# Hedgehog linear attention, twice and mixed: phase 2 with token-major queries, a DMA exchange and 32x32 array tiles

## The chip, the cores and the metric

The kernel runs on one core of one Trainium2 chip. The metric is the time of one execution on the device in microseconds; lower is better. Engines are called as in the profile: PE (TensorE matmuls), PEld (its weight loads), DVE (VectorE), ACT (ScalarE), POOL (GpSimd) and SP (SyncE, which here only issues DMAs).

## The reference, cut to what matters

Two linear attentions, A and B, run over the same input x of 2048 tokens and 448 features, with 16 heads of 28 features each. The outputs are mixed by a gate per token.

```python
def _ref(x, wqkv, w_phi, wo):                 # once with A's weights, once with B's
    q, k, v = split(x @ wqkv)                 # each (heads, tokens, 28)
    pq = einsum("hsd,hdf->hsf", q, w_phi);  pk = einsum("hsd,hdf->hsf", k, w_phi)
    phi_q = concat([softmax(pq), softmax(-pq)]);  phi_k = concat([softmax(pk), softmax(-pk)])
    kv = einsum("hsf,hsd->hfd", phi_k, v);  z = einsum("hsf->hf", phi_k)
    num = einsum("hqf,hfd->hqd", phi_q, kv)
    den = einsum("hqf,hf->hq", phi_q, z)[..., None] + 1e-6
    return merge_heads(num / den) @ wo
g = sigmoid((x * gate_w).sum(-1, keepdims=True))
out = g * a + (1 - g) * b
```

## The kernel before, in words

Everything is 32-bit. x lies transposed in SBUF (features on partitions, tokens along the free axis) as a high and a low part, and so do the projection weights, so that a product is a sum over 11 chunk pairs: seven with the high weights, four with the low ones. w_phi is folded into the k and q weights first (`fold`), so the projections give pk and pq at once. The tokens are cut into 16 tiles of 128.

The order of the work is written out by hand: each engine runs its instructions in the order in which the program lists them, and waits on semaphores for the others. Nothing is rescheduled.

**Phase 1**, for each tile t: k projection (`proj`, 22 matmuls of 448 columns: tokens on the output's partitions), the two softmaxes on DVE, ACT and POOL (`k_soft`: shift by the maximum and the minimum, exponentials, sums, reciprocals, products), v projection with the gate's logit as an extra column (`v_out`), and the accumulation of phi_k^T v of the tile before (`kv_acc`). In `kv_acc` the outputs of four heads lie on the four column strips of the array (29 rows each at partitions 0, 32, 64, 96), and all sums stay in one PSUM bank over the 16 tiles. The q weights are folded in tiles 6 to 9, wo is loaded in tile 11.

**Phase 2** makes q feature-major: `q_mm` takes the weights as the stationary operand (128 padded features, 32 to a head, four heads to a block) and 256 tokens as the moving one. A unit is two such blocks for 256 tokens, 44 matmuls for the two units of a tile; `q_shift` turns it by 32x32 blocks on DVE, reduces, and POOL subtracts; `q_done` is the exponential (ACT) and the turn back (DVE, into eT). `num` multiplies eT by the block-diagonal kvbd, four heads at a time, 8 matmuls for each of A and B, with 30 columns a head: 28 numerators, the sum for the denominator, and the softmax's own sum. `weigh` and `combine` work out the weights (DVE), multiply the numerators (DVE) and add the two halves (POOL). `out_turn` turns the result by seven TensorE transposes, `out_split` makes its high and low parts (ACT, DVE), `out_mm` is the output projection of 21 matmuls of 448 columns, `out_end` copies and stores. Tile t's loop body holds the q units of a later tile, the numerators of tile t, and the output of tile t - 1.

PSUM has eight banks: two of one bank (`one`), and in phase 1 three of two banks (`two`), which phase 2 gives to the numerators and the transposes. The DMAs all go through SP's queue, in program order.

Of the kernel before, what the change touches and what calls it, by code (L numbers as in the profile page):

```python
# [23 lines left out]
TB = 256  # L24
MC = 30
WARM = 16


@with_exitstack
def hedgehog_mix(ctx: ExitStack, tc: tile.TileContext, xd, wv, wkt, wqt, wphi, wo, cmask, cpmask, out):  # L30
# [9 lines left out]
    ident = const.tile([P, P], F32, name="ident")  # L40
    make_identity(nc, ident)
    mask = const.tile([PF, 4], F32, name="mask")
    pmask = const.tile([P, 4], F32, name="pmask")
    xg = [const.tile([P, 7, GT], F32R, name=f"xg{g}") for g in range(NG)]
    glog = const.tile([P, NT], F32, name="glog")
    gate = const.tile([P, NT, 2], F32, name="gate")

    work = ctx.enter_context(tc.tile_pool(name="work", bufs=2))
    wt_pool = ctx.enter_context(tc.tile_pool(name="wt", bufs=1, side="right"))
    start = ExitStack()  # L50
    raw = start.enter_context(tc.tile_pool(name="raw", bufs=1, side="right"))
    ph1 = ExitStack()
    wk_pool = ph1.enter_context(tc.tile_pool(name="wkv", bufs=1))
    wp = wk_pool.tile([PF, 2, 4, HP], F32, name="wp")
    bd = wk_pool.tile([PF, 2, 4, P], F32, name="bd")
    wkh = wk_pool.tile([P, 4, 2 * D], F32R, name="wkh")
    wkl = wk_pool.tile([P, 4, 2 * D], F32R, name="wkl")
    wvh = wk_pool.tile([P, 4, VC], F32R, name="wvh")
    wvl = wk_pool.tile([P, 4, VC], F32R, name="wvl")
    NV = 3  # L60
    vs = [wk_pool.tile([P, 2, NP, 2, DH + 1], F32, name=f"vs{i}") for i in range(NV)]


# [17 lines left out]
    def load_wt(src, n):  # L81
        wt = wt_pool.tile([P, 4096], F32, name="wt")[:PF].rearrange("p (b g c) -> p b g c", b=2, g=4)
        for c in range(0, 512, n):
            for b in range(2):
                nc.sync.dma_start(wt[:, b, :, c:c + n], src[b, :, c:c + n].rearrange("(g p) c -> p g c", p=PF))  # L85
        return wt
# [15 lines left out]
    load_x_rest(0, P, 2 * P, GT)  # L102
    nc.sync.dma_start(pmask, cpmask)
    for v in vs:
        nc.gpsimd.memset(v[:, :, :, :, DH:], 1.0)
    for q in range(4):
        nc.vector.tensor_scalar(bd[:, :, :, q * HP:(q + 1) * HP], wp, mask[:, q:q + 1], None, op0=OP.mult)

    def fold(c, wt, wh, wl, w):
        n = 4 * w  # L110
        ps = two.tile([P, 2, 512], F32, name="two")
        for b in range(2):
            for g in range(4):
                nc.tensor.matmul(ps[:, b, g * n:(g + 1) * n], wt[:, b, g, c * P:(c + 1) * P],  # L114
                                 bd[:, b, g].rearrange("p (q f) -> p q f", f=HP)[:, :, :w], start=True, stop=True)
        dh = wh[:, c, :].rearrange("p (b f) -> p b f", b=2)
        dl = wl[:, c, :].rearrange("p (b f) -> p b f", b=2)
        nc.scalar.activation(dh, ps[:, :, :4 * n], AF.Copy)
        nc.vector.tensor_tensor(dl, ps[:, :, :4 * n], dh.bitcast(F32), OP.subtract)

    def proj(t, wh, wl, name, widths):
        ps = two.tile([P, 2, 512], F32, name="two")
# [15 lines left out]
    def shift(ps):  # L138
        p4 = hb(ps[:, :, :D])
        mx = wk_pool.tile([P, 2, 2, H], F32, name="mx", bufs=2)  # L140
        e = wk_pool.tile([P, 2, HA * DH], F32, name="e", bufs=2)
# [8 lines left out]
    def expo(e):  # L150
        for s in range(2):
            nc.scalar.activation(e[:, s], e[:, s], AF.Exp)  # L152
        return e

    def k_soft(ps):
        e = expo(shift(ps))
        sm = wk_pool.tile([P, 2, HA], F32, name="sm", bufs=2)
        rs = wk_pool.tile([P, 2, HA], F32, name="rs", bufs=2)
# [14 lines left out]
    kvp = one.tile([P, 512], F32, name="one")  # L173
    nc.vector.memset(kvp, 0.0)
    kvp = kvp[:, :HA * DH // 2].rearrange("p (b g s f) -> p b g s f", b=2, g=4, f=DH)
# [310 lines left out]
```

## Time and profile before

| what | value |
|---|---|
| time, median of 3 runs | 416.81 us (415.45 to 416.84) |
| profiled execution: time | 416.56 us |
| profiled execution: span | 414.5 us |
| busy PE, PEld, DVE, ACT, POOL | 404.6, 380.6, 308.3, 124.9, 187.5 us |
| granted TensorE clock | 0.996 of full speed |
| DMA | 15.62 MB, 38 GB/s on average |

The span runs from the program's first instruction to its last; the time is taken from outside and is some 2 us longer. Busy times are the union of an engine's instructions. In a row of a group the columns are line, engine, operation, output<-inputs with the shapes, the count, then after the first bar the busy time in us and the mean duration of one in ns, and after the second bar the idle time of the engine just before and what ended it. A row of the chain has start and length in us, engine, tile and line. A row of a window has, per engine, the busy us and the number of instructions, then the granted clock, the DMA share and GB/s.

### The profile page before, as it was taken

Reading aid. Unit: us, or ns where it says so; the run is one execution under the profiler, and the core shown is the slowest. Engines: PE = TensorE matmul, PEld = TensorE weight load, DVE = VectorE, ACT = ScalarE, POOL = GpSimd, SP = SyncE. Lnnn points to the kernel's source line nnn. Section 1 sums busy time; section 2 is a strip of 40 time slices with the busy share of each in tenths; the row PEclk is TensorE's granted clock in tenths of the full one; section 3 lists DMA queues with packets and bytes.
Section 4 is the critical chain, followed back from the end, with each engine's and each line's share of the span. In section 5 each row is a group of like instructions: output and inputs, shape, how many; then the busy total and the mean of one; then the engine's idle time right before and its main releaser. Section 6 shows DMA issues by size and latency. Waiting matters only on the chain.

```text
span 414.5 us, 8240 instructions
## 1 busy us (share of the span) xinstructions
PE 404.6 (98%) x3536; PEld 380.6 (92%) x3536; DVE 308.3 (74%) x453; ACT 124.9 (30%) x162; POOL 187.5 (45%) x159
## 2 busy tenths in 40 slices
PE   8999999999999999999799999999999999999996
PEld 7898888899998888899699999999999999999995
DVE  2776666666676666678899987888788878888961
ACT  2624242423332222225432322132213221322212
POOL 0375565643321333338865636443644364436321
PEclk9999999999999999999989999999999999999999
DMA  8845306000000000000000000000000000000001
GB/s 182 287 130 150 103 2 252 7 2 2 2 2 2 2 2 2 2 0 3 1 2 22 24 0 24 24 22 2 24 23 24 0 24 24 23 2 24 23 24 44
DMA packets 12036, 15.62 MB, mean 38 GB/s; under 512 B 880, under 2 KB 9056, under 8 KB 12000
## 3 DMA queue, kind: packets, MB, share of 16 engines
q1 hardware_dynamic: 12000, 15.10, 11.7%
q8 instruction: 28, 0.46, 0.5%
q14 instruction: 8, 0.07, 0.1%
HBM read 11.43 MB, written 3.67 MB: 36 GB/s over the span
## 4 chain that ended last, share of the span: by engine, by line
PE 86%; DVE 6%; ACT 2%; POOL 2%; DMA 2%; SPq 1%; issue 1%; POOLq 0%; DVEq 0%; ACTq 0%
PE two L130 34%; PE one L240 17%; PE one L371 16%; PE nb L323 6%; PE na L323 6%; PE one L184 3%; PE turn L354 3%; PE two L114 2%; DMA xraw<-in_xt 2%; DVE eT L262 1%; SPq L85 1%; DVE ctt L347 1%; DVE sm L160 1%; DVE qmx L250 0%; ACT wt L258 0%
## 5 line engine op out<-in xcount | busy, mean ns | idle before, releaser
L164 POOL TENSOR_TENSOR e<-e,rs 128x896 f32<-128x896 f32 x32 | 53.8, 1703 | 92.9 <-DVE rs L161 92.9
L349 POOL TENSOR_TENSOR o<-ctt 128x448 f32<-128x448 f32 x32 | 36.3, 1152 | 76.1 <-PE one L371 49.3
L152 ACT ACTIVATE e<-e 128x896 f32<-128x896 f32 x32 | 30.2, 955 | 106.7 <-DVE e L146 106.6
L240 PE MATMUL one<-xg,wqh 128*128 128x256 f32 x392 | 56.8, 285 | 0.0
L130 PE MATMUL two<-wkh,xg 128*128 128x448 f32 x224 | 52.5, 372 | 0.7 <-POOL xg L79 0.4
L142 DVE TENSOR_REDUCE mx<-two 128x32 f32<-128x896 f32 x16 | 17.5, 1091 | 47.8 <-PE two L130 47.8
L240 PEld LDWEIGHTS one<-xg,wqh 128*128 128x128 f32 x392 | 52.3, 193 | 0.4
L130 PE MATMUL two<-wvh,xg 128*128 128x450 f32 (+1 forms) x224 | 51.4, 369 | 0.0
L253 POOL TENSOR_TENSOR wt<-wt,qmx 128x512 f32<-128x512 f32 x32 | 33.6, 1049 | 32.4 <-DVE qmx L250 32.4
L130 PEld LDWEIGHTS two<-wkh,xg 128*128 128x128 f32 x224 | 40.8, 188 | 5.5 <-POOL xg L79 0.7
L130 PEld LDWEIGHTS two<-wvh,xg 128*128 128x128 f32 x224 | 42.4, 189 | 3.7
L358 ACT ACTIVATE oh<-turn 128x896 fp32r<-128x896 f32 (+2 forms) x17 | 14.8, 873 | 101.0 <-DVE cdd L336 79.2
L262 DVE STREAM_TRANSPOSE eT<-wt 128x1024 f32<-128x1024 f32 x32 | 39.4, 1233 | 2.1 <-ACT wt L258 2.1
L258 ACT ACTIVATE wt<-wt 128x1024 f32<-128x1024 f32 x32 | 32.5, 1052 | 12.6 <-POOL wt L254 12.6
L240 PE MATMUL one<-xg,wql 128*128 128x256 f32 x224 | 36.0, 283 | 0.0
L160 DVE TENSOR_REDUCE sm<-e 128x32 f32<-128x896 f32 x32 | 33.3, 1081 | 1.3
L323 PE MATMUL nb<-kvbd,eT 128*128 128x120 f32 x256 | 31.4, 275 | 2.7 <-DVE eT L262 2.7
L254 POOL TENSOR_TENSOR wt<-qmx,wt 128x512 f32<-128x512 f32 x32 | 33.5, 1048 | 0.0
L323 PEld LDWEIGHTS nb<-kvbd,eT 128*128 128x128 f32 x256 | 29.9, 192 | 2.9 <-DVE eT L262 2.9
L323 PE MATMUL na<-kvbd,eT 128*128 128x120 f32 x256 | 31.2, 275 | 0.3 <-POOL kvbd L310 0.3
L130 PE MATMUL two<-wvl,xg 128*128 128x450 f32 (+1 forms) x128 | 31.4, 367 | 0.0
L130 PE MATMUL two<-wkl,xg 128*128 128x448 f32 x128 | 31.1, 364 | 0.0
(75 smaller groups left out, 686.7 us busy)
## 6 DMA issues: line engine op xcount, KB each, us to landing
out<-ob SPq DMA_DIRECT2D x16, 224.0 KB, 1.9
xraw<-in_xt SPq DMA_DIRECT2D x3, 1024.0 KB, 5.5
wvr<-in_wv SPq DMA_DIRECT2D x4, 449.0 KB, 6.8
wt<-in_wkt SPq DMA_DIRECT2D x8, 224.0 KB, 5.5
wt<-in_wqt SPq DMA_DIRECT2D x2, 896.0 KB, 9.5
wor<-in_wo SPq DMA_DIRECT2D x1, 1568.0 KB, 10.4
xraw<-in_xt SPq DMA_DIRECT2D x2, 256.0 KB, 7.3
xraw<-in_xt SPq DMA_DIRECT2D x1, 512.0 KB, 8.6
```

Of the source, the lines that this page charges most:

```text
L130: nc.tensor.matmul(ps[:, b, :n], x[:, xc, o:o + P], w[:, wc, lo:lo + n], start=i == 0, stop=i == len(terms) - 1)
L152: nc.scalar.activation(e[:, s], e[:, s], AF.Exp)
L160: nc.vector.tensor_reduce(sm[:, s], e[:, s].rearrange("p (h f) -> p h f", f=DH), AX.X, OP.add)
L164: nc.gpsimd.tensor_tensor(e3, e3, rs[:, s, :, None].to_broadcast([P, HA, DH]), OP.mult)
L240: nc.tensor.matmul(ps[:, i * TB:(i + 1) * TB], w[:, wc, lo:lo + P], x[:, xc, o:o + TB], start=n == 0, stop=n == len(terms) - 1)
L253: nc.gpsimd.tensor_tensor(ep[:, :512].rearrange("p (j f) -> p j f", f=HP), t3, bc[0], OP.subtract)
L254: nc.gpsimd.tensor_tensor(ep[:, 512:].rearrange("p (j f) -> p j f", f=HP), bc[1], t3, OP.subtract)
L258: nc.scalar.activation(ep, ep, AF.Exp)
L262: nc.vector.transpose(eT.rearrange("p s i t -> p (s i t)"), ep)
L323: nc.tensor.matmul(ps[:, s, g * 120:(g + 1) * 120], eTs[t // 2, 2 * b + g // 2][:, s, g % 2, o:o + P], kvbd[:, b, s, g].rearrange("p h m - ...
L349: nc.gpsimd.tensor_tensor(o[:, (lo + b) * D:(lo + b + 1) * D], tt[:, 0].rearrange("p a f -> p (a f)"), tt[:, 1].rearrange("p a f -> p (a f ...
L371: nc.tensor.matmul(ps[:, :D], a, w, start=first and i == 0, stop=last and i == len(terms) - 1)
```

## The change

Phase 2 is rebuilt, and with it the hand-over from phase 1.

- q is projected like k: tokens on partitions, 22 matmuls of 448 columns a tile (`proj` into `qps`). `q_shift` subtracts the maximum, into uq.
- `q_swap` exchanges partitions and head groups: 16 DMAs from SBUF to SBUF, each 32 partitions of 896 bytes. After it partition 32r + j holds head group r of the tokens 32c + j, c along the free axis. uq has one buffer, the target tq two.
- `q_exp0` and `q_exp1` (ACT) and `q_min` (DVE, POOL) make the two softmaxes' exponentials; `q_turn` turns 32x32 blocks on DVE, so that features lie on partitions, 32 to a head group.
- `num` runs in 32x32 tiles of the array: for each of A and B, each softmax, each column strip g and each row strip r a matmul of 32 rows, 32 columns and 128 tokens. Its 64 outputs fill four PSUM banks, row strip r in bank r. There is no block-diagonal kvbd any more.
- `n_turn` turns all of it back on DVE; `n_rec` and `n_mix` work out the weights, with the products and the sum on POOL; `o_turn` turns the result on DVE (before: TensorE transposes); `o_hi` and `o_lo` split it on ACT and POOL. The heads now lie in another order, so wo's rows are permuted once by two DMAs within DRAM (wos) and loaded in seven parts at the end of phase 1.
- The gate is exchanged as q is, by 16 small DMAs for tiles 0 to 12 and 16 for the last three.
- q projections run four tiles ahead (LEAD): tiles 0 and 1 in phase 1's tiles 12 and 13, tiles 2 and 3 behind phase 1. The q weights are folded in tiles 2 to 5. Buffers are shared over the phases, and vs has two buffers instead of three.

The core of the diff, with the new functions:

```diff
@@ kv_acc
-                    h = 4 * g + r
+                    h = 4 * r + g
@@ new
+    def q_shift(k, ps):
+        mx = work.tile([P, 2, H], F32, name="qmx")
+        p4 = hb(ps[:, :, :D])
+        nc.vector.tensor_reduce(mx, p4, AX.X, OP.max)
+        for b in range(2):
+            nc.vector.tensor_tensor(uq[:, :, b], p4[:, b].rearrange("p (r g) f -> p r g f", r=4),
+                                    mx[:, b].rearrange("p (r g) -> p r g", r=4)[:, :, :, None].to_broadcast([P, 4, 4, DH]),
+                                    OP.subtract)
+    def q_swap(k):
+        tr = trs[k] = tq[k % 2]
+        for r in range(4):
+            for c in range(4):
+                nc.sync.dma_start(tr[32 * r:32 * r + 32, c], uq[32 * c:32 * c + 32, r])
+    def q_exp0(k):
+        nc.scalar.activation(eq[:, 0, :, :, :DH], tview(k), AF.Exp)
+    def q_min(k):
+        mn = work.tile([P, 4, 8], F32, name="qmn")
+        nc.vector.tensor_reduce(mn, trs[k].rearrange("p c b g f -> p c (b g) f"), AX.X, OP.min)
+        nc.gpsimd.tensor_tensor(eq[:, 1, :, :, :DH], mn.rearrange("p c a -> p a c")[:, :, :, None].to_broadcast([P, 8, 4, DH]),
+                                tview(k), OP.subtract)
+    def q_exp1(k):
+        nc.scalar.activation(eq[:, 1, :, :, :DH], eq[:, 1, :, :, :DH], AF.Exp)
+    def q_turn(k):
+        eT = wtb[:, 2048 * (k % 2):2048 * (k % 2) + 2048]
+        eTs[k] = eT.rearrange("p (s b g t) -> p s b g t", s=2, b=2, g=4)
+        nc.vector.transpose(eT, eq.rearrange("p s a c f -> p (s a c f)"))
+    def gates(lo, hi):
+        gl = glog[:, lo:hi]
+        nc.scalar.activation(gl, gl, AF.Exp, scale=-1.0)
+        nc.vector.tensor_scalar(gl, gl, 1.0, None, op0=OP.add)
+        nc.vector.reciprocal(gl, gl)
+        for r in range(4):
+            for c in range(4):
+                nc.sync.dma_start(gate[32 * r:32 * r + 32, 0, c, lo:hi], glog[32 * c:32 * c + 32, lo:hi])
+        nc.gpsimd.tensor_scalar(gate[:, 1, :, lo:hi], gate[:, 0, :, lo:hi], -1.0, 1.0, op0=OP.mult, op1=OP.add)
@@ phase 1, in the loop over t (tile 0: the rows of wo are permuted in DRAM)
+            w5 = wos.rearrange("g (r b f) n -> b g r (f n)", r=4, b=2)
+            for b in range(2):
+                nc.sync.dma_start(w5[b], wo[b * D:(b + 1) * D, :].rearrange("(r g f) n -> g r (f n)", r=4, g=4))
...
+        if 2 <= t < 6:
+            fold(t - 2, wt, wqh, wql)
...
+        if t == NT - 4:
+            gates(0, t + 1)
+        if t in (QT - 2, QT - 1):
+            k = t - QT + 2
+            q_shift(k, proj(k, wqh, wql, (D, D), two_tile()))
+            q_swap(k)
+        if t in (QT - 1, QT):
+            k = t - QT + 1
+            q_exp0(k)
+            q_min(k)
+            q_exp1(k)
+            q_turn(k)
@@ between the phases
+    for k in (2, 3):
+        q_shift(k, proj(k, wqh, wql, (D, D), two_tile()))
+        q_swap(k)
     kv_acc(NT - 1, phi.pop(NT - 1))
+    for b in range(2):
+        nc.scalar.activation(kvs[:, b, :, :, :DH], kvp[:, b].rearrange("p g s f -> p s g f"), AF.Copy)
+    nc.vector.transpose(kvt..., kvs...)
+    nc.gpsimd.memset(kvt[:, :, :, :, DH + 1], 1.0)
...
+    for c in range(7):
+        nc.sync.dma_start(wor[c], wos[:, HP * c:HP * (c + 1), :])
+    gates(NT - 3, NT)
@@ phase 2
+    def num(i):
+        ps = nps.tile([P, 4, 4, P], F32, name="num")
+        for b in range(2):
+            for s in range(2):
+                for g in range(4):
+                    for r in range(4):
+                        nc.tensor.matmul(ps[32 * g:32 * g + 32, r, 2 * b + s], kvt[32 * r:32 * r + 32, b, s, g],
+                                         eTs[i][32 * r:32 * r + 32, s, b, g], start=True, stop=True)
+    def n_turn(i, ps):
+        nc.vector.transpose(cb[i % 2][:, :2048], ps.rearrange("p r a t -> p (r a t)"))
+    def n_rec(i):                                # 64 values each
+        nc.vector.reciprocal(rs, cv[:, :, :, :, DH + 1])
+        nc.gpsimd.tensor_tensor(dd, cv[:, :, :, :, DH], rs, OP.mult)
+    def n_mix(i):
+        nc.vector.scalar_tensor_tensor(den..., dd[:, :, 0], 1e-6, dd[:, :, 1], op0=OP.add, op1=OP.add)
+        nc.vector.reciprocal(den, den)
+        nc.gpsimd.tensor_tensor(den, den, gate[:, None, :, :, i].to_broadcast([P, 4, 2, 4]), OP.mult)
+        nc.gpsimd.tensor_tensor(dd, rs, den..., OP.mult)
+        nc.gpsimd.tensor_tensor(c3, c3, dd...to_broadcast([P, 64, DH]), OP.mult)
+        nc.gpsimd.tensor_tensor(o..., c4[:, :, 0, :, :DH], c4[:, :, 1, :, :DH], OP.add)
+    def o_turn(i):
+        nc.vector.transpose(oTs[i % 2].rearrange("p k (c t) -> p k c t", c=4), o)
+    def o_hi(i):
+        nc.scalar.activation(hl[:, 0], oTs[i % 2], AF.Copy)
+    def o_lo(i):
+        nc.gpsimd.tensor_tensor(hls[i][:, 1], oTs[i % 2], hls[i].bitcast(F32)[:, 0], OP.subtract)
+    for i in range(NT + 2):
+        if i == 0:
+            pq = q_proj(LEAD)
+            split_wo(0, 4)
+        if i < NT:
+            ps = num(i)
+        if 0 < i < NT - LEAD:
+            pq = q_proj(i + LEAD)
+        if i < NT:
+            n_turn(i, ps)
+            n_rec(i)
+        if i + 2 < NT:
+            q_exp0(i + 2)
+            q_min(i + 2)
+        if 0 < i <= NT:
+            o_turn(i - 1)
+            o_hi(i - 1)
+        if i + 2 < NT:
+            q_exp1(i + 2)
+        if i < NT:
+            n_mix(i)
+        if 0 < i <= NT:
+            o_lo(i - 1)
+        if i + LEAD < NT:
+            q_shift(i + LEAD, pq)
+            q_swap(i + LEAD)
+        if i + 2 < NT:
+            q_turn(i + 2)
+        if i == 0:
+            split_wo(4, 7)
+        if i >= 2:
+            out_end(i - 2, out_mm(i - 2))
```

350 lines of the change are left out of this document (108 added, 242 removed).

## The prediction

> **What bounds the kernel now.** I read the page's busy line first, then the chain that ended last in order of time, then one window of the second phase, then the groups for durations.
>
> ```profile
> PE 404.6 (98%) x3536; PEld 380.6 (92%) x3536; DVE 308.3 (74%) x453; ACT 124.9 (30%) x162; POOL 187.5 (45%) x159
> ```
>
> ```profile
> 162.19 9.16 PE two L130 x44
> 172.28 4.66 PE two L130 x22
> 176.96 1.09 DVE mx L142
> ...
> 217.54 4.27 PE one L371 x21
> 221.81 5.21 PE one L240 x44
> 227.01 1.78 PE na L323 x16
> 229.56 1.78 PE nb L323 x16
> 231.34 4.27 PE one L371 x21
> 235.61 5.21 PE one L240 x44
> ```
>
> ```profile
> 280.00:320.00 40.00, 40.00 (x302) 39.05 (x301) 33.21 (x57) 10.07 (x12) 18.43 (x18) 1.00 0.04 14
> ```
>
> TensorE has no spare time. A tile of phase 1 takes 10.09 us (162.19 to 172.28), one of phase 2 takes 13.80 (221.81 to 235.61): q projection 5.21, numerators twice 1.78, output 4.27, and 0.77 between na and nb (227.01 + 1.78 to 229.56), the transposes. In the window PE, DVE, ACT and POOL are busy 40.00, 33.21, 10.07 and 18.43 of 40 us, which is 2.9 tiles: 11.5 on DVE and 6.4 on POOL per tile, so both follow PE with room.
>
> **The change, per tile of 128 tokens.** Durations for what comes:
>
> ```profile
> 181.37 0.99 PE L184 MATMUL one<-e,vs 128*29 128x56 f32 x64
> ...
> 182.33 1.07 PE L240 MATMUL two<-xg,wqh 128*128 128x256 f32 x7
> ```
>
> ```profile
> L164 POOL TENSOR_TENSOR e<-e,rs 128x896 f32<-128x896 f32 x32 | 53.8, 1703 | 92.9 <-DVE rs L161 92.9
> L253 POOL TENSOR_TENSOR wt<-wt,qmx 128x512 f32<-128x512 f32 x32 | 33.6, 1049 | 32.4 <-DVE qmx L250 32.4
> L349 POOL TENSOR_TENSOR o<-ctt 128x448 f32<-128x448 f32 x32 | 36.3, 1152 | 76.1 <-PE one L371 49.3 <-DVE ctt L347 26.7
> L79 POOL TENSOR_TENSOR xg<-xraw,xg 128x1536 fp32r<-128x1536 f32 x3 | 10.6, 3527 | 0.2
> L94 POOL TENSOR_TENSOR wol<-wor,woh 128x448 fp32r<-128x448 f32 x7 | 7.9, 1141 | 0.0
> L262 DVE STREAM_TRANSPOSE eT<-wt 128x1024 f32<-128x1024 f32 x32 | 39.4, 1233 | 2.1 <-ACT wt L258 2.1
> L248 DVE STREAM_TRANSPOSE wt<-one 128x512 f32<-128x512 f32 x28 | 19.9, 711 | 12.9 <-PE one L240 12.9
> L142 DVE TENSOR_REDUCE mx<-two 128x32 f32<-128x896 f32 x16 | 17.5, 1091 | 47.8 <-PE two L130 47.8
> L161 DVE RECIPROCAL rs<-sm 128x64 f32<-128x64 f32 x16 | 8.9, 554 | 0.6
> L342 DVE RECIPROCAL cden<-cden 128x32 f32<-128x32 f32 x12 | 4.2, 353 | 0.4
> L336 DVE TENSOR_TENSOR cdd<-nb,crs 128x32 f32<-128x32 f32 x16 | 3.1, 192 | 0.5
> L152 ACT ACTIVATE e<-e 128x896 f32<-128x896 f32 x32 | 30.2, 955 | 106.7 <-DVE e L146 106.6
> L358 ACT ACTIVATE oh<-turn 128x896 fp32r<-128x896 f32 x15 | 13.8, 917 | 95.2 <-DVE cdd L336 79.2 <-PE turn L354 16.0
> L375 ACT ACTIVATE ob<-one 128x448 f32<-128x448 f32 x16 | 8.7, 544 | 46.9 <-PE one L371 46.9
> ```
>
> ```profile
> 0.74 0.40 SPq L96 DMA_DIRECT2D wp<-in_wphi  x1
> 1.19 0.41 SPq L97 DMA_DIRECT2D mask<-in_cmask  x1
> 1.65 4.90 SPq L85 DMA_DIRECT2D wt<-in_wkt  x8
> ```
>
> ```profile
> out<-ob SPq DMA_DIRECT2D x16, 224.0 KB, 1.9
> wor<-in_wo SPq DMA_DIRECT2D x1, 1568.0 KB, 10.4
> ```
>
> *PE.* The q projection becomes that of phase 1: 22 matmuls, half of 9.16, so 4.58 for 5.21. The seven transposes (0.77) go. The numerators become 64 matmuls in 32x32 tiles, 128 instructions of 128 columns, since a 32-bit matmul counts twice (na: 8 matmuls, x16). Their time N is unknown. Upper end, one after another: 1.78/16 = 0.111 us for 120 columns, so 128 x 0.111 x 128/120 = 15.2. For tiles the nearest row is the accumulation at L184, whose outputs lie on four column strips: 64 instructions from 181.37 to 182.33, 15 ns each for 56 columns, where 0.111 x 56/120 = 52 ns would be a full pass; four strips bring 3.5-fold. If the four row strips bring nothing, N = 15.2/3.5 = 4.4; if all sixteen run perfectly, 0.95. The loop has the row strip innermost and gives each its own PSUM bank; I take 3.5 x 3.5 = 12, N = 1.3. PE per tile: 4.58 + 4.27 + 1.3 = 10.15 for 13.80. Over 16 tiles that is 58 us less PE work.
>
> The Trainium skill (TensorE: Matmul & The Clock Gate, Part 3, on row and column tiling) gives 10.6-fold for sixteen such tiles in bf16; by it N would be 1.4, an estimate, and the sum 1 us longer. No row here shows row strips.
>
> *POOL.* From L253 and L164 an operation with a broadcast operand costs 0.18 + 1.70 ns per element; from L349 and L79 one with two full operands 0.18 + 2.19 ns. The minimum's subtraction (896): 1.70. Weighing the numerators (1792, broadcast): 3.22. Adding the two halves (896): 2.14. The low part o_lo (896): 2.14. Three small ones of 32 or 64: 0.9. Sum 10.1, before 6.4.
>
> *DVE.* From L262 a transpose costs 0.19 + 1.02 ns per element (PSUM alike, L248). n_turn 2.3, q_turn 2.3, o_turn 1.1, reductions 2 x 1.09, two shifts of 448 at 0.63, reciprocals 0.55 and 0.35, one small 0.19. Sum 10.2, before 11.5.
>
> *ACT.* 2 x 0.955 + 0.917 + 0.544 = 3.4, hidden.
>
> *SP.* q_swap issues 16 DMAs of 28 KB per tile. An issue on a quiet queue takes 0.40 and the next follows 0.45 to 0.46 after it; in the burst of wkt 4.90/8 = 0.61. The bounds are 0.33 (the store of ob lies there) and 0.61:
>
> ```profile
> L376 SPq DMA_DIRECT2D out<-ob x16: 332/333/362, 223.2 to 411.8; - x16
> ```
>
> I take 0.42, because each moves only 32 rows: 6.7 us, and 1.9 to land as for out. The source uq has one buffer, so the next tile's shifts (1.25) wait for the landing: this loop is 9.9 per tile. Queued behind the swap on SP is the store of the output, which has a tile of slack.
>
> *At nothing.* The folds of wq move from tiles 6 to 9 to tiles 2 to 5; their weights were asked for in tile 0, two phase-1 tiles (20 us) ahead; if they came later, PE would wait at tile 2. Reordering wo in DRAM puts two DMAs ahead of x's third load on SP, which tile 8 needs first. The first gate DMAs (16 x 0.42 and 1.9 to land, 8.6) hold POOL in tile 12 in front of phi(13), which has 10 us. Gone are the pmask copies into kvbd on ACT, beside other work already. With two instead of three vs buffers ACT's copy waits for the accumulation of two tiles before, long done.
>
> So four loops lie at 10.15, 10.1, 10.2 (some 0.07 less for each DVE operation, whose successor starts before it ends: 9.6) and 9.9. Phase 2's period is at least 10.15; with every hand-over late by 0.1 it is 10.6. I take 10.4.
>
> **The hand-over between the phases.** Two q projections move into phase 1: the k projection of the last tile ends at 176.96 + 9.2 = 186.1. On DVE the transpose q_turn(1) stands ahead of the last softmax. It waits for POOL: phi(14), then its own subtraction, then ACT. From the end of k projection 14 (176.0): q_turn(0) holds DVE until 179.9, softmax 14 until 186.7 (6.9), phi(14) 3.4, subtraction 1.7, exponential 1.0, q_turn 2.3: 195.1. Softmax 15 to 202.0, phi(15) to 205.4, and the last accumulation at 205.5. In between PE does q projections 2 and 3, then q 4 until 211.0. q_shift(2) ends at 204.1; its swap has landed at 204.1 + 6.7 + 1.9 = 212.8; only then q_shift(3) ends (214.1), kvt is turned, and num(0) starts at 215.0.
>
> Now SP: swap(3) until 220.9, seven loads of wor until 224.0, 16 small gate DMAs until 230.7, landing 232.6. The wor rows pass through the same queue: 10.4 after 220.9 if as before. POOL's gate operation waits for the gate DMAs, and behind it on POOL stand four splits of wo (4 x 1.14) and then everything of tile 0. I let wor and gates be in at 237 (16 us: between 10.4 and four times that, near the row). Then: splits 241.8, den on DVE 242.6, q_shift(4) 244.8. Only now may q projection 5 write its single PSUM buffer: PE stands from 220.1 (after num 1) to 244.8, 25 us. Projection 5, num 2 (6 us), q_shift(5) after o_turn(0) (4 us of splits and turn), projection 6: the first output matmul starts about 18 us after that, at 262.8; before, 217.5.
>
> **The sum.** Outputs 0 to 9 are one period apart: 262.8 + 9 x 10.4 = 356.4. The next four have no projection beside them, but POOL still has 10.1 for two and 8.2 for two, plus 1.2 of waiting: 37.8, so output 13 starts at 394.2. From the last num, which ends 3.2 before that: n_turn and reciprocal 2.9, POOL and DVE to the end of the addition 7.3, o_lo(14) 2.1, two outputs 8.5, copy 0.55, store 0.33 + 1.9, end 0.4: 24, that is 21 after output 13 starts. Span 415.2. The profiled execution of before had a span of 414.5 and a time of 416.56, 2.06 more; its three runs have median 416.81. So 417.3, say 417: 58 us of PE work are saved, and nearly all of it is lost again in standing PE, some 40 us at the hand-over and some 20 at the end.
>
> **Rivals.** Under 0.5%, about 2 us, can't be told from no change here: faster means below 414.7, slower above 418.9.
> - *The gain comes through* (0.24): wor lands after 10.4 and the loops never trip, so the first output starts at 258.6 and the period is 10.15: 258.6 + 91.3 + 37.8 + 21 = 408.7, with 2.1: 411. For it speaks that busy POOL and DVE rows follow each other with no gap now. It decides from first output + 9 periods below 353.6.
> - *Row strips do not run side by side* (0.13): N = 4.4, PE 13.25 per tile. 9 x 2.85 = 26 more, and some 3 in the last tiles: 446. It decides from N = 2: each 0.1 beyond 1.55 adds 1 us. This one ends on the other side, as do the next.
> - *The exchange sets the period* (0.14): an issue of 0.50 makes the loop 16 x 0.50 + 1.9 + 1.25 = 11.2: 9 x 0.8 = 7, and three swaps in the hand-over at 1.3: 428; at 0.61, 449. It decides from 0.46.
> - *wor comes on few DMA engines* (0.09). The page gives what all engines did:
>
> ```profile
> q1 hardware_dynamic: 12000, 15.10, 11.7%
> ```
>
> 15.1 MB in 0.117 x 16 x 414.5 us is 19.5 GB/s for one engine; its source is cut into 4 groups of rows. On four engines 1.6 MB would take 20.6 + 1.9, in at 243.4, 6.4 later: 424. The Trainium skill (DMA: Bandwidth & Descriptors, on how many engines a DMA uses) says it takes the largest count up to 16 that divides both sides' slowest dimension, here 4; by that rule this case holds. All loads before have the same rows on both sides, so no run shows it.
> - *The forecast* (0.40): 412 to 424, of which 0.10 below 414.7, 0.13 within, 0.17 above.
>
> Faster 0.24 + 0.10 = 0.34; same 0.13; slower 0.17 + 0.13 + 0.14 + 0.09 = 0.53. The range leaves out the end of the gain and the far ends of N and of the issue: 406 to 442. The forecast's own is 412 to 424.
>
> **What would show it.** Right: matmuls at num of 1.0 to 1.6 us per tile; outputs 10.2 to 10.6 apart while projections run; POOL over 95% busy there; PE idle over 20 us around 220 to 245, ended by DVE's q_shift behind POOL's gate operation; SP at 0.42 per swap DMA. Wrong: num above 2 us; shifts of q waiting for the exchange in each tile; half-rate clock in phase 2; first output before 250 or after 270.

## The result and the profile after

| what | before | after |
|---|---|---|
| time, median | 416.82 us (415.45 to 416.91) | 479.64 us (477.94 to 480.93) |
| ratio, 95% interval | | 1.1513 (1.147 to 1.1557) |
| profiled execution: span | 414.5 us | 477.6 us |
| granted clock, mean | 0.996 | 0.907 |
| first output matmul, us from the start | 217.5 | 288.1 |
| mean distance of outputs 0 to 9 | 13.8 | 13.7 |

The kernel is 15% slower, beyond the predicted range. The output matmuls start 11.0, 13.7, 16.4, 11.1, 13.8, 16.9, 11.4, 16.2 and 12.6 us apart: the same mean pace as before, though PE now has some 10.8 us of work per tile, and 70.6 us later.

The page of the changed kernel: busy time by engine, then the chain that ended last, by engine and by line.

```profile
PE 376.8 (79%) x4608; PEld 332.4 (70%) x4608; DVE 288.9 (60%) x293; ACT 121.3 (25%) x158; POOL 247.0 (52%) x177
...
SPq 33%; PE 31%; DMA 11%; DVE 9%; POOL 8%; issue 5%; ACT 1%; DVEq 0%; POOLq 0%; ACTq 0%
SPq L202 27%; PE two L130 24%; DMA tq<-uq 6%; DVE uq L194 3%; SPq L244 3%; DMA wvh<-wos 3%; PE one L380 2%; PE one L181 2%; POOL e L373 2%; PE two L115 1%; DMA xrb<-in_xt 1%; POOL wvl L359 1%; POOL vs L362 1%; DVE sm L157 1%; SPq L314 1%
```

Before, the chain was 86% PE. Now a third of it is SP's queue, nearly all in L202, the swap: 27% of 477.6 is 129 us of issuing, with another 6% for landing. Which waits this makes (engine and line, what it waits for, total us, times, longest):

```profile
PE q L130 <- DVE uq L194: 68.4, 12, 32.5
...
POOL gate L245 <- DMA gate<-glog: 45.0, 2, 36.3
DVE uq L194 <- DMA tq<-uq: 44.4, 11, 8.8
```

Read from the bottom: the shifts (L194) wait 44.4 us for the swap of the tile before to land, since uq has one buffer; PE's q projection (L130) waits for these shifts, its PSUM buffer being single too. The middle row is the hand-over. The swap itself (duration of an issue, min/median/max, in ns):

```profile
L202 SPq DMA_DIRECT2D tq<-uq x256: 507/589/1777, 164.4 to 431.3; - x128
```

The starts of two issues in a row lie 0.633 us apart (median). One turn of the loop, from the order of time (start, us, engine and line):

```profile
306.87 1.16 DVE L194 TENSOR_TENSOR uq<-q,qmx 128x448 f32<-128x448 f32 x2 [3.29 <-DMA tq<-uq]
...
308.17 10.89 SPq L202 DMA_DIRECT2D tq<-uq  x16
...
321.74 1.16 DVE L194 TENSOR_TENSOR uq<-q,qmx 128x448 f32<-128x448 f32 x2 [4.49 <-DMA tq<-uq]
```

Shift, 16 issues, the landing of the last (318.46 to 321.62 in the chain), next shift: 14.87 us in this turn, and DVE stands idle for 4.49 of it. The least a turn can take is 15 x 0.633 to the last issue, 1.8 to land, 1.17 of shifts and 0.1 between: 12.6; longer landings (to 3.9) and, in half of the loop's bursts, one late issue bring the mean to 13.7.

The hand-over, by SP's queue alone:

```profile
153.76 10.55 SPq L244 DMA_DIRECT2D gate<-glog  x16
164.41 67.09 SPq L202 DMA_DIRECT2D tq<-uq  x64
231.61 2.60 SPq L314 DMA_DIRECT2D wvl<-wos  x4
234.25 1.59 SPq L314 DMA_DIRECT2D wvh<-wos  x1
235.88 2.15 SPq L314 DMA_DIRECT2D wvl<-wos  x1
238.08 2.22 SPq L314 DMA_DIRECT2D wvh<-wos  x1
240.41 16.05 SPq L244 DMA_DIRECT2D gate<-glog  x16
```

The last of the four swaps that stand ahead of the weights leaves SP at 231.5, then come the seven loads of wor, then the 16 gate DMAs. The chain shows what that ended in (start, us, what):

```profile
238.08 12.80 DMA wvh<-wos
251.45 0.59 SPq L244
...
255.88 1.70 DMA gate<-glog
258.05 4.35 POOL wkl L97 x4
```

The last wor load landed at 250.9. Three of the gate issues stand 2.4 us apart in SP's queue (246.19, 248.57, 250.90), the pace at which the wor loads landed, and only then the rest go out at 0.63. The gates were in at 257.6, POOL's gate operation had waited 36.3, and behind it stood the splits. What the engines did meanwhile (after the window's length, busy us of PE, PEld, DVE, ACT, POOL; then clock, DMA share, GB/s):

```profile
240.00:260.00 20.00, 0.00 (x0) 0.00 (x0) 0.00 (x0) 1.99 (x3) 2.15 (x3) 0.50 0.15 50
```

No matmul for 20 us, and the clock at half. The groups of phase 2 (busy us, mean ns | idle before):

```profile
L222 DVE STREAM_TRANSPOSE wtb<-xrb 128x2048 f32<-128x2048 f32 x16 | 36.9, 2304 | 9.3 <-ACT xrb L217 9.3
L333 PE MATMUL num<-wtb,kvt 32*32 32x128 f32 x2048 | 32.6, 297 | 2.4 <-DVE wvh L339 2.4
L213 POOL TENSOR_TENSOR xrb<-qmn,tq 128x896 f32<-128x896 f32 x16 | 28.1, 1759 | 14.5 <-DVE qmn L212 13.9 <-DMA tq<-uq 0.6
...
L359 POOL TENSOR_TENSOR wvh<-wvh,cdd 128x1792 f32<-128x1792 f32 x8 | 25.7, 3218 | 0.6
...
L362 POOL TENSOR_TENSOR vs<-wvl 128x896 f32<-128x896 f32 x8 | 16.8, 2099 | 0.6
```

These are the costs of the work itself, and none of them made the kernel slow.

### The profile page after: what moved, and what is told of

It is laid out like the page before. It is cut to its first block, busy times and chain, and to the rows that moved or that the text cites. A ratio compares the mean times of both kernels' runs of the same rounds, so it can differ in the third digit from the quotient of the medians.

```text
span 477.6 us, 10643 instructions
## 1 busy us (share of the span) xinstructions
PE 376.8 (79%) x4608; PEld 332.4 (70%) x4608; DVE 288.9 (60%) x293; ACT 121.3 (25%) x158; POOL 247.0 (52%) x177
## 4 chain that ended last, share of the span: by engine, by line
SPq 33%; PE 31%; DMA 11%; DVE 9%; POOL 8%; issue 5%; ACT 1%; DVEq 0%; POOLq 0%; ACTq 0%
SPq L202 27%; PE two L130 24%; DMA tq<-uq 6%; DVE uq L194 3%; SPq L244 3%; DMA wvh<-wos 3%; PE one L380 2%; PE one L181 2%; POOL e L373 2%; PE two L115 1%; DMA xrb<-in_xt 1%; POOL wvl L359 1%; POOL vs L362 1%; DVE sm L157 1%; SPq L314 1%
## 5 line engine op out<-in xcount | busy, mean ns | idle before, releaser
L161 POOL TENSOR_TENSOR e<-e,rs 128x896 f32<-128x896 f32 x32 | 53.8, 1703 | 93.6 <-DVE rs L158 87.0
L130 PE MATMUL q<-wqh,xg 128*128 128x448 f32 x168 | 47.7, 432 | 68.4 <-DVE uq L194 68.4
L130 PEld LDWEIGHTS q<-wqh,xg 128*128 128x128 f32 x168 | 37.3, 228 | 75.0 <-issue 36.8
L380 PE MATMUL one<-wkh,e 128*128 128x448 f32 x224 | 57.0, 400 | 16.6 <-POOL e L373 15.6
L380 PEld LDWEIGHTS one<-wkh,e 128*128 128x128 f32 x224 | 45.8, 208 | 23.6 <-POOL e L373 17.5
L130 PE MATMUL two<-wvh,xg 128*128 128x450 f32 (+1 forms) x224 | 51.0, 366 | 2.5 <-DVE e L147 2.5
L130 PE MATMUL two<-wkh,xg 128*128 128x448 f32 x224 | 52.1, 370 | 0.9 <-POOL xg L82 0.4
L130 PEld LDWEIGHTS two<-wvh,xg 128*128 128x128 f32 x224 | 42.0, 188 | 6.2 <-issue 2.8
L130 PEld LDWEIGHTS two<-wkh,xg 128*128 128x128 f32 x224 | 40.9, 188 | 5.3 <-POOL xg L82 0.7
L222 DVE STREAM_TRANSPOSE wtb<-xrb 128x2048 f32<-128x2048 f32 x16 | 36.9, 2304 | 9.3 <-ACT xrb L217 9.3
L194 DVE TENSOR_TENSOR uq<-q,qmx 128x448 f32<-128x448 f32 x24 | 13.9, 620 | 38.3 <-DMA tq<-uq 31.2
L352 DVE SCALAR_TENSOR_TENSOR cden<-cdd 128x32 f32<-128x32 f32 x16 | 16.6, 1041 | 33.7 <-POOL cdd L348 33.7
L213 POOL TENSOR_TENSOR xrb<-qmn,tq 128x896 f32<-128x896 f32 x16 | 28.1, 1759 | 14.5 <-DVE qmn L212 13.9
L208 ACT ACTIVATE xrb<-tq 128x896 f32<-128x896 f32 x16 | 15.2, 952 | 79.8 <-DVE wtb L222 66.4
L333 PE MATMUL num<-wtb,kvt 32*32 32x128 f32 x2048 | 32.6, 297 | 2.4 <-DVE wvh L339 2.4
L333 PEld LDWEIGHTS num<-wtb,kvt 32*32 32x32 f32 x2048 | 25.9, 107 | 9.8 <-issue 4.0
L130 PE MATMUL two<-wvl,xg 128*128 128x450 f32 (+1 forms) x128 | 31.1, 365 | 0.0
L130 PE MATMUL two<-wkl,xg 128*128 128x448 f32 x128 | 30.8, 362 | 0.0
L130 PE MATMUL q<-wql,xg 128*128 128x448 f32 x96 | 26.8, 407 | 0.0
## 6 DMA issues: line engine op xcount, KB each, us to landing
wtb<-in_wkt SPq DMA_DIRECT2D x8, 224.0 KB
out<-wvh SPq DMA_DIRECT2D x8, 224.0 KB
out<-wvl SPq DMA_DIRECT2D x8, 224.0 KB
```

Source lines behind the costliest of these rows:

```text
L130: nc.tensor.matmul(ps[:, b, :n], x[:, xc, o:o + P], w[:, wc, lo:lo + n], start=i == 0, stop=i == len(terms) - 1)
L161: nc.gpsimd.tensor_tensor(e3, e3, rs[:, s, :, None].to_broadcast([P, HA, DH]), OP.mult)
L194: nc.vector.tensor_tensor(uq[:, :, b], p4[:, b].rearrange("p (r g) f -> p r g f", r=4), mx[:, b].rearrange("p (r g) -> p r g", r=4)[:, :, ...
L213: nc.gpsimd.tensor_tensor(eq[:, 1, :, :, :DH], mn.rearrange("p c a -> p a c")[:, :, :, None].to_broadcast([P, 8, 4, DH]), tview(k), OP.sub ...
L222: nc.vector.transpose(eT, eq.rearrange("p s a c f -> p (s a c f)"))
L333: nc.tensor.matmul(ps[32 * g:32 * g + 32, r, 2 * b + s], kvt[32 * r:32 * r + 32, b, s, g], eTs[i][32 * r:32 * r + 32, s, b, g], start=True ...
```

## The experiments

The theory after the result: the 16 issues of a swap, at 0.633 and not 0.42, make the loop through the single uq the period, and the same queue is the hand-over. The rivals: the exchange costs by its bytes or landing, not by its issues; or the hand-over is held by something else.

### One DMA for the swap

```diff
-        for r in range(4):
-            for c in range(4):
-                nc.sync.dma_start(tr[32 * r:32 * r + 32, c], uq[32 * c:32 * c + 32, r])
+        nc.sync.dma_start(tr, uq)
```

> Leaves out the permuting: q_swap copies all of uq to tq by one DMA, the same bytes in one issue instead of sixteen, so the heads and tokens are mixed up while every other instruction stays. Theory (issue): the changed kernel is held by SP, which needs 0.633 us for each of the 16 DMAs; a loop of 16 x 0.633 + 2.4 landing + 1.2 shifts = 13.7 us per tile, and four swaps in a row in the hand-over. Then the period falls to PE's own 4.6 + 4.3 + 1.9 = 10.8 to 11.2, the first output starts some 40 us earlier, and the time is 414 to 422. Rival (bytes): the 0.46 MB per tile through the DMA engines set the time; then nothing changes, 475 or more. Rival (hand-over of wo's rows): the period falls but the first output hardly moves, 440 to 450.

424.53 us, ratio 1.0177 (1.0149 to 1.0206): 55 us of the 63 are gone with the same bytes. The period is 10.9 nine times. The first output starts at 262.9, which is 25 us earlier and not some 40. The one issue per tile:

```profile
L200 SPq DMA_DIRECT2D tq<-uq x16: 465/471/537, 163.9 to 364.9; - x16
```

The time is 2.5 us above the expectation, but both rivals are out, the bytes and the rows of wo: the number of issues is the cost, not the 448 KB. This kernel leaves the permuting out; the exchange through DRAM below keeps it.

### A second uq buffer

From tile 5 on the odd tiles use another buffer; the 16 DMAs stay.

```diff
+    def uqb(k):
+        if k < 5 or k % 2 == 0:
+            return uq
+        return cb[1][:, 2048:2944].rearrange("p (r b g f) -> p r b g f", r=4, b=2, g=4)
...
-                nc.sync.dma_start(tr[32 * r:32 * r + 32, c], uq[32 * c:32 * c + 32, r])
+                nc.sync.dma_start(tr[32 * r:32 * r + 32, c], uqb(k)[32 * c:32 * c + 32, r])
```

> A second buffer for uq in every odd tile from 5 on (in the place of the second oT, which is then single). Theory (issue, and one source buffer): the landing of 2 to 4 us and the shifts drop out of the loop, SP issues without a break, 16 x 0.633 + 0.4 = 10.6 per tile, PE needs 10.8: period 11 instead of 13.7 over ten tiles, 25 us less, 450 to 458; the hand-over is as it was. Rival (the issue alone): PE and POOL wait just as long for the exchange two tiles later, less than 8 us gained. Rival (bytes): no change.

455.63 us, ratio 1.0949 (1.0904 to 1.0994), as expected. The first output hardly moves (285.1); the outputs 0 to 9 lie 10.8 to 12.5 apart, 11.1 in the mean. So in the loop it is not the sum of the issues alone (10.1 to 10.9 per tile) but their sum with landing and shift, in series through one buffer.

### Half of the DMAs from ACT's queue

```diff
-                nc.sync.dma_start(tr[32 * r:32 * r + 32, c], uq[32 * c:32 * c + 32, r])
+                (nc.sync if r < 2 else nc.scalar).dma_start(tr[32 * r:32 * r + 32, c], uq[32 * c:32 * c + 32, r])
```

> Half of the 16 swap DMAs are issued from ACT's queue. Theory (issue): each queue needs 8 x 0.633 = 5.1 us, the loop is 5.1 + 2.4 + 1.2 = 8.7, so the period is PE's 10.8 to 11.5, with ACT at 3.4 + 5.1 = 8.5 us per tile; the hand-over's four swaps take 20 us less: 425 to 435. Rival (one generator behind both queues): the two queues share what writes the descriptors, each issue takes twice as long, 470 to 480. Rival (bytes): no change.

444.15 us, ratio 1.0646 (1.0615 to 1.0676): a miss by 9 us. The two queues do issue side by side (medians 0.592 on SP and 0.603 on ACT), and the period falls to 11.1 to 11.4. But ACT's issues wait for the shifts like SP's, and ACT's own work stands behind them. In these rows most of the wait is ACT's own issuing, which the trace counts as idle: eight issues from 303.88 to 310.20, then the copy at 310.24.

```profile
ACT wvl L385 <- DMA tq<-uq: 39.8, 5, 8.7
...
ACT wvh L385 <- DMA tq<-uq: 31.6, 4, 8.6
```

The first output starts at 277.6, 15 us later than with one DMA. Moving issues to an engine that has work of its own moved a wait there too.

### The exchange through DRAM, with five issues

```diff
+        ud = uds[k % 2]
+        nc.sync.dma_start(ud, uq)
         for r in range(4):
-            for c in range(4):
-                nc.sync.dma_start(tr[32 * r:32 * r + 32, c], uq[32 * c:32 * c + 32, r])
+            nc.sync.dma_start(tr[32 * r:32 * r + 32].rearrange("j c b g f -> j c (b g f)"),
+                              ud[:, r].rearrange("(c j) b g f -> j c (b g f)", c=4))
```

> The same exchange by way of DRAM: one store of uq and four loads of 32 partitions, each with 4 x 896 bytes; 5 issues per tile in place of 16, twice the bytes, two landings. Theory (issue): 5 x 0.4 to 0.63 = 2.0 to 3.2 us of SP, uq is free 2.5 us after the shift, tq is complete 7 us after it, which a tile's 11 us cover: period 10.8 to 11.3, hand-over some 35 us shorter, 415 to 425. Rival (bytes): slower than the changed kernel, 485 or more.

428.23 us, ratio 1.0271 (1.0243 to 1.0299), 3 us above the expectation. It moves every byte twice and still gives back 51 us. The period is 10.9, and PE has no gap in it. SP's queue, in the loop:

```profile
248.24 0.35 SPq L202 DMA_DIRECT2D ud<-uq  x1
252.72 1.73 SPq L204 DMA_DIRECT2D tq<-ud  x4
```

2.1 us of issuing instead of 10. What is left above the kernel before is the hand-over; in order of time:

```profile
239.09 0.20 POOL L248 TENSOR_SCALAR gate<-gate 128x12 f32<-128x12 f32 x1 [31.71 <-DMA gate<-glog]
239.25 4.38 POOL L98 TENSOR_TENSOR wkl<-wvl,wkh 128x448 fp32r<-128x448 f32 x4
...
248.26 1.11 PE L131 MATMUL q<-wqh,xg 128*128 128x448 f32 x2 [29.97 <-DVE uq L195]
```

POOL waited 31.71 for the gates, and PE stood 29.97.

### The last gates later

On top of the exchange through DRAM.

```diff
-    gates(NT - 3, NT)
...
+        if i == 4:
+            gates(NT - 3, NT, mix=False)
+        if i == 6:
+            gate_mix(NT - 3, NT)
```

> The kernel with the exchange bounced through DRAM (1 store and 4 loads), and in addition the second group of gate DMAs issued in iteration 4 of the loop and its POOL operation in iteration 6, instead of both ahead of phase 2. Theory (in the hand-over POOL waits for the 16 gate DMAs that are queued behind the seven loads of the output weights, and PE waits for POOL): POOL can go on at about 226.9, after the four splits of weights that landed by 225.1, instead of 243.6, so about 16.5 us less than the bounced kernel's 428.2: 411 to 413. Rival (the hand-over is held by something else, the exchange or the splits of the weights): no change, 426 to 428.

412.89 us, ratio 0.9923 (0.99 to 0.9946), as expected: 15.3 us less. POOL now goes from the last of the first four splits straight on, and PE stands 14 instead of 30:

```profile
226.54 1.13 POOL L98 TENSOR_TENSOR wkl<-wvl,wkh 128x448 fp32r<-128x448 f32 x1 [1.24 <-ACT wkh L97]
227.63 0.35 POOL L354 TENSOR_TENSOR cdd<-wvh,crs 128x64 f32<-128x64 f32 x1
...
232.31 2.98 PE L131 MATMUL q<-wqh,xg 128*128 128x448 f32 x7 [14.12 <-DVE uq L195]
```

### The output weights earlier as well

The seven loads, and the buffers they need, stand ahead of q projections 2 and 3.

```diff
+    woh = wp_.tile([P, 7, D], F32R, name="wkh")
...
+    for c in range(7):
+        nc.sync.dma_start(wor[c], wos[:, HP * c:HP * (c + 1), :])
     for k in (2, 3):
         q_shift(k, proj(k, wqh, wql, (D, D), two_tile()))
         q_swap(k)
```

> As the kernel with late gates, and in addition the buffers of the output weights taken and their seven loads issued ahead of q projections 2 and 3, so that they land by about 208 instead of 225 and later. Theory (what remains of the hand-over is the loading of the weights and their splits on POOL): splits done at about 212, the first products of phase 2 at about 216, the projection q of tile 4 can start at about 220 instead of 248: 27 to 28 us less than the bounced kernel, 400 to 403, ratio to the kernel before about 0.96. Rival (POOL or VectorE holds the hand-over whatever the loads do): about 410, the same as with late gates alone.

409.01 us, ratio 0.9823 (0.9805 to 0.9842): 3.9 us less and not 10 to 13. It is below the kernel before, but nearer to the rival's 410. The splits now start at 212.8 and are done at 217.3, not at 212, because POOL's small fill of kvt, ahead of them, waits 7.27 for DVE. PE's wait falls to 2.3 us at tile 5, but 6.6 come at tile 6, and the first output starts at 247.1, only 4.1 earlier. Why, in order of time:

```profile
212.72 0.13 POOL L321 MEMSET kvt<- 128x16 f32 x1 [7.27 <-DVE kvt L320]
...
231.81 1.13 POOL L98 TENSOR_TENSOR wkl<-wvh,wkh 128x448 fp32r<-128x448 f32 x1
232.91 1.12 POOL L98 TENSOR_TENSOR wkl<-wvl,wkh 128x448 fp32r<-128x448 f32 x1
...
234.00 1.12 POOL L98 TENSOR_TENSOR wkl<-wvh,wkh 128x448 fp32r<-128x448 f32 x1
...
235.08 0.34 POOL L354 TENSOR_TENSOR cdd<-wvl,crs 128x64 f32<-128x64 f32 x1
...
239.85 2.95 PE L131 MATMUL q<-wqh,xg 128*128 128x448 f32 x7 [6.62 <-DVE uq L195]
```

The other three splits stand on POOL ahead of tile 1's denominators, behind which DVE's next shift stands. The expectation had moved only the first wait. In the loop PE is the bound (one window):

```profile
260.00:280.00 20.00, 20.00 (x335) 17.47 (x334) 19.46 (x19) 5.01 (x8) 18.05 (x12) 1.00 0.37 117
```

### The hand-over alone, with the 16 DMAs kept

The loads of the last section and the gates of the one before it, put into the changed kernel.

```diff
+    for c in range(7):
+        nc.sync.dma_start(wor[c], wos[:, HP * c:HP * (c + 1), :])
     for k in (2, 3):
...
-    gates(NT - 3, NT)
...
+        if i == 4:
+            gates(NT - 3, NT, mix=False)
```

> The changed kernel with its 16 swap DMAs per tile kept as they are; only the loads of the output weights are earlier and the second gates later, as in the kernel with early weights. Theory (hand-over and exchange are two separate losses that add): the projection q of tile 4 starts at about 234 instead of 267, the period of a tile stays at 13.7, about 32 us less than the changed kernel: about 447. Rival (while the exchange holds the loop, the hand-over is worth nothing): 475 to 480.

456.58 us, ratio 1.0962 (1.0926 to 1.0998): 23 us less than the changed kernel, not 32. The first output comes at 257.4, 30.7 earlier, as the theory has it; but the outputs 0 to 9 are then 14.8 apart in the mean. One step, from 312.3 to 333.2, is 20.9; SP's queue before it:

```profile
291.52 10.25 SPq L202 DMA_DIRECT2D tq<-uq  x16
301.88 0.52 SPq L389 DMA_DIRECT2D out<-wvh  x1
302.50 11.03 SPq L244 DMA_DIRECT2D gate<-glog  x16
313.70 10.69 SPq L202 DMA_DIRECT2D tq<-uq  x16
```

The late gates cost the full queue 11.0 us; in the kernels that exchange through DRAM the queue has room for them. So the two losses are separate causes, but they do not simply add: the fix of the one needs the room that the other leaves.

### The strips in the other order

```diff
-                for g in range(4):
-                    for r in range(4):
+                for r in range(4):
+                    for g in range(4):
```

> As the kernel with early weights, and in addition the 128 small matmuls of the numerators ordered with the column strip innermost instead of the row strip. Theory (the order with row strips innermost holds the small matmuls at 13 to 15 ns each): the numerators fall from 1.6 to about 0.9 us, the period of a tile from 10.9 to about 10.2, some 6 us less than the kernel with early weights. Rival (the order does not matter, each small matmul costs the same): the same time as the kernel with early weights within 1 us.

410.43 us, ratio 0.9846 (0.9827 to 0.9864), beside 409.01 for the kernel it is built on. 128 matmuls take 1.63 us from the first start to the last in either order, and their group is unchanged (292 ns for one, before 293):

```profile
L339 PE MATMUL num<-wtb,kvt 32*32 32x128 f32 x2048 | 32.1, 292 | 2.4 <-DVE wvh L345 2.4
```

The period is 10.86 in both. The times overlap (409.2 to 410.67 beside 408.72 to 410.23), though the medians lie 1.4 apart and the rival had said 1. The rival holds: the order is worth nothing.

### What an issue costs, by form

Four forms of the exchange in one kernel, by tile.

```diff
+        if k % 4 == 0:    # (0) 16 x tr[32 * r:32 * r + 32, c] <- uq[32 * c:32 * c + 32, r]
+        elif k % 4 == 1:  # (1)  4 x tr[:, r] <- uq[:, r]
+        elif k % 4 == 2:  # (2) 16 x ud[32 * c:32 * c + 32, r] <- uq[32 * c:32 * c + 32, r], then 4 loads
+        else:             # (3) ud <- uq, then 16 x tr[32 * r:32 * r + 32, c] <- ud[32 * c:32 * c + 32, r]
```

> The kernel with early output weights, with four forms of exchange in turn, by tile number modulo 4: (0) 16 DMAs of 32 rows from SBUF to SBUF, as in the changed kernel; (1) four DMAs of 128 rows from SBUF to SBUF, the permuting left out; (2) 16 stores of 32 rows to DRAM and four loads of 128 rows; (3) one store and 16 loads of 32 rows. To be read: the time from issue to issue in SP's queue for each form. Theory A (the price goes by where the data come from and go to): 0.60 to 0.63 for (0) and for (1), 0.34 for each store of (2), 0.43 for each load of (3). Theory B (the prediction's choice: a DMA of few rows is cheaper): below 0.34 for the stores of (2) and below 0.43 for the loads of (3), and (1) above (0). Theory C (a DMA of 32 rows is dear wherever it goes): 0.60 for (0), (2) and (3), and 0.43 to 0.47 for (1).

The four lines in order, (0) to (3), duration of one issue in ns:

```profile
L205 SPq DMA_DIRECT2D tq<-uq x64: 507/589/1608, 163.8 to 346.9; - x64
...
L208 SPq DMA_DIRECT2D tq<-uq x16: 510/599/1822, 177.0 to 352.6; - x16
...
L213 SPq DMA_DIRECT2D ud<-uq x64: 302/419/1565, 207.4 to 369.1; - x64
...
L222 SPq DMA_DIRECT2D tq<-ud x64: 313/419/1748, 222.2 to 383.5; - x64
```

From start to start 0.63 for (0) and 0.64 for (1), whether 32 rows or 128; 0.46 for the stores of (2) and the loads of (3). Theory A holds in its order: with both ends in SBUF an issue is dearer by 0.17, and the number of rows plays no part; B and C fall. A's own figures for 32 rows to and from DRAM (0.34 and 0.43) were low; in a row of issues both are 0.46. Larger loads from DRAM go at another pace: in the kernel before, the eight loads of wkt (224 KB each) start 0.53 apart. The time, 431.44 in one execution, says nothing beyond that. Why the ends matter stays open.

### All seven splits together

On top of the early weights.

```diff
-            split_wo(0, 4)
+            split_wo(0, 7)
...
-        if i == 0:
-            split_wo(4, 7)
```

> The kernel with early output weights, and the last three of the seven splits of the output weights done together with the first four, ahead of the first products, instead of in the middle of iteration 1. Theory (what is left of the hand-over is POOL: those three splits of 1.12 each hold up the denominators of tile 1 from 231.8 to 235.1, while POOL stands idle for 5.7 ahead of 223.1): 3.4 us less, 405 to 406. Rival (VectorE's own work sets the start of the loop): the same as with early weights, 408 to 410.

406.41 us, ratio 0.9737 (0.97 to 0.9773) beside 0.9823 with early weights alone; 0.4 above the expectation. The first output moves from 247.1 to 244.1, and tile 1's denominators from 235.08 to:

```profile
232.61 0.36 POOL L354 TENSOR_TENSOR cdd<-wvl,crs 128x64 f32<-128x64 f32 x1
```

This is the fastest version here: the same mathematics as the change, 73 us faster than it and 10 us faster than the kernel before.

### VectorE takes work of POOL's in the tail

```diff
-        nc.gpsimd.tensor_tensor(hls[i][:, 1],
+        (nc.vector if i >= 12 else nc.gpsimd).tensor_tensor(hls[i][:, 1],
...
-        nc.gpsimd.tensor_tensor(o.rearrange(
+        (nc.vector if i >= 13 else nc.gpsimd).tensor_tensor(o.rearrange(
```

> As the kernel with all seven splits together, and in the tail, where no projection runs, two of POOL's operations go to VectorE: the low half of the outputs (POOL 2.10) from tile 12 on, and the sum of the two products (POOL 2.12) from tile 13 on. Theory (from 350 on POOL is at 10.1 us per tile and PE waits for it, 14.4 us in all): per tile POOL falls to about 6 to 8 and the tail is 6 to 9 us shorter, 397 to 400, ratio to the kernel before about 0.955. Rival (in the tail the chain through all engines sets the pace, not POOL's sum of work): 0 to 3 us, 402 to 406.

408.21 us (406.56 to 408.74), ratio 0.9782 (0.9758 to 0.9807), beside 406.41 (404.34 to 407.54) without it: no gain, and above even the rival's 402 to 406. In the two profiled executions the spans are the same (404.8 and 404.7): the first output comes 3.0 earlier here, where nothing was changed, so that much is chance. But from the start of output 9 to that of the last it takes 56.4 us instead of 53.8, and 52.5 to 54.3 in the other kernels with a cheap exchange and a period of 10.9. Each operation is half as long on DVE, 1.09 for 2.1, but it now waits there for POOL's long product, and the next tile's n_turn waits behind it:

```profile
369.57 1.09 DVE L368 TENSOR_TENSOR vs<-wvl 128x896 f32<-128x896 f32 x1 [4.05 <-POOL wvl L365]
...
373.81 2.27 DVE L345 STREAM_TRANSPOSE wvh<-num 128x2048 f32<-128x2048 f32 x1
...
376.75 0.35 POOL L354 TENSOR_TENSOR cdd<-wvh,crs 128x64 f32<-128x64 f32 x1 [7.21 <-DVE crs L353]
```

POOL, relieved, waits 7.21 for DVE. The tail is a chain through both engines, as the rival said.

## Why the prediction was wrong

The span was forecast at 415.2 and was 477.6, 62.4 more. By the prediction's own three terms: the first output at 288.1 instead of 262.8 (25.3), nine periods of 123.1 instead of 93.6 (29.5), and from output 9 to the end 66.4 instead of 58.8 (7.6).

**The step that failed is the price of a swap issue.** "I take 0.42, because each moves only 32 rows" was a choice between 0.33 and 0.61, taken from loads and stores with one end in DRAM. It is 0.633, above both ends of its bounds, and the reason was false: rows play no part, both ends in SBUF do, and the trace of before had no such DMA. Nor was 0.61 the pace of a burst: the eight issues of wkt start 0.53 apart, and the last alone took 1.23. The prediction also said from where this decides, 0.46; that is what even the cheaper kind costs in a burst. The rival "the exchange sets the period", given 0.14, is what happened, in its place and by its mechanism. Its price by its own formula, 16 x 0.633 + 1.9 + 1.25 = 13.3, is near the 13.7 measured. But it priced only the loop and three swaps of the hand-over, and so ended at 449 for 0.61.

**What it left out lies on the same queue.** The gates' 32 DMAs go at the same price: the first 16 took 10.55 and not 6.7. The seven loads of wor took 8.7 to issue and not 3.1. The second gate group took 16.05, since three of its issues went out 2.4 us apart, the pace at which the wor loads landed (ACT's splits behind these loads start at 236.74, 239.11 and 241.48). So swap 3 left SP at 231.5 (forecast 220.9), the wor issues at 240.3 (224.0), the gates at 256.5 (230.7), in at 257.6, not at the 232.6 of the queue's sum nor at the 237 taken. The mechanism of the hand-over was right to the row: POOL's gate operation, behind it the splits, DVE's shift behind those, and PE idle until then. The late gates took away nearly what the theory said, 15.3 us of 16.5; the early weights gave only 3.9 more of the 10 to 13 expected.

**A hit by luck.** The forecast's first output at 262.8 was met by the one-DMA kernel, at 262.9, and so was the shift at 244.8, behind which PE goes on there at 244.82. But there the last swap left SP before 208.3 and not at 220.9, and the second gates took 17.7 us and not 6.7: two errors that cancel.

**wor on few DMA engines** was the rival with 0.09, and it holds. The first load was issued at 231.6 and the last landed at 250.9, 19.3 us, where the forecast had 16 in its sum and 10.4 as the nearest row. From 240.0 to 250.9, while wor was still coming, the DMA share is 0.26, and 0.26 x 16 is 4.2 engines. The Trainium skill (DMA: Bandwidth & Descriptors, on how many engines a DMA uses) gives four; by that rule the trace agrees. On the time it acted through SP's queue: the gates landed last, and 5.5 of the 16.05 us of their issuing are what the first 16 did not need.

**N** was sized at 1.3 and is 1.63 from the first start to the last, 1.9 with the end of the last. That is 9.3-fold against the 15.2 of one after another, not the 12 taken. The Trainium skill (TensorE: Matmul & The Clock Gate, Part 3) has 10.6-fold, in a row that names no data type; the estimate of 1.4 from it was the nearer one. The row strips do run side by side, so the rival of 446 is out. In the changed kernel N cost little, as PE wasn't the bound; in the kernels with a cheap exchange it is why the period is 10.9 (4.6 + 4.27 + 1.9, and some 0.1) and not the 10.4 forecast.

**"One small 0.19" in DVE's sum** is cden, and it took more. Beside POOL's subtraction of the minimum it took 1.0 to 1.7 us and ended within 0.05 us of it, 14 times of 16; the two times without that neighbour it took 0.19 (min, median, max in ns):

```profile
L352 DVE SCALAR_TENSOR_TENSOR cden<-cdd x16: 193/1008/1732, 262.7 to 457.8; 128x32 f32<-128x32 f32 x16
```

So DVE's 9.6 was 10.6 per tile in the loop of the kernel with early weights (19.46 of 20 us). There it did not set the pace, since PE was busy throughout; in the hand-over it ended 2.1 after the splits and not 0.8. No run here tests what stretches it.

**The end** was 7.6 longer than forecast. In the one-DMA kernel it is 62.5, so 3.9 of that is the exchange: the last swap is issued until 431.9. The other 3.7 was not taken apart; some matmuls there ran at half the clock (see the last section).

Of the forecast's own signs of being wrong three came: shifts that wait for the exchange, the half-rate clock, and a first output after 270.

**Right:** the durations on POOL and DVE (3.22 for 3.22, 2.10 for 2.14, 1.76 for 1.70, 2.30 for 2.3) and ACT under cover. Once the exchange is cheap, four loops at about the same length do run with few trips: 10.8 to 10.9 nine times in the kernel with early weights, with POOL some 90% (forecast over 95%) and DVE 97% busy. The end, forecast 58.8 from output 9, is 62.9 in the fastest kernel.

So the gain forecast as a rival (411 by cheap loads and loops that do not trip) can be had, but not with 16 SBUF-to-SBUF DMAs per tile.

## What to carry to other kernels

Price a DMA's issue by its form, both ends included, and take the pace within a burst, not the duration of one on a quiet queue. Multiply by all the DMAs that the change puts on that queue, and where a buffer is single, close the loop: issues, landing and refill add up, and are compared with the period. Before moving work to an engine with free time, look at what it would wait for there and what stands behind it in that engine's order: half the swap on ACT and the tail's sums on DVE each paid back less than the sums of work promised, or nothing.

## What the runs showed of the hardware

- Start to start in a burst on SP's queue: 0.63 for a DMA from SBUF to SBUF, of 32 or 128 rows, 0.46 with one end in DRAM (28 KB each; 0.53 for the 224 KB loads of wkt). In the changed kernel nine of the 16 swap bursts have a late issue, 0.5 to 1.2 us more; what makes it isn't known.
- Issues can stand still behind slow transfers: three gate DMAs went out 2.4 us apart while wor loads landed at that pace, in the changed kernel, and in the same way in the four others in which the gates follow wor at once (16 to 18 us for 16 issues). With wor earlier or the gates later the same 16 went out in 10 to 11 us.
- The clock falls while PE stands: 0.50 from 240 to 260, and in four-us windows still 0.50 up to 272 with PE busy again. Seven q matmuls took 2.98 us at 267.0 and 1.68 at 308.2. One of these windows, with PE busy throughout:

```profile
268.00:272.00 4.00, 4.00 (x12) 3.57 (x11) 3.97 (x4) 0.95 (x1) 3.92 (x3) 0.50 0.15 33
```

  The Trainium skill (TensorE: Matmul & The Clock Gate, Part 1) has half rate after an idle window of some 3.4 us and until a busy one is over. The long stand and the pauses of 3.98 to 5.46 us in this kernel agree: seven matmuls behind them took 2.16 to 2.98 us. A shorter pause can cost the same: seven output matmuls took 2.98 at 423.03 after 2.46 us of idling, while after 2.80 and 2.86 seven q matmuls took 1.68 and 1.67. A forecast of a standing PE should add this to the wait.
